# 112 unread f16 matmuls into spare PSUM columns, in front of 27 instructions of the attention stage

## The chip, the cores and the metric

The kernel runs on one core of a Trainium2 chip. The time is that of the device, in microseconds (us), from launch to end; less is better. TensorE (PE) does the matmuls and the transposes, VectorE (DVE), ScalarE (ACT) and GpSimd (POOL) work on their results, and SyncE (SP) issues transfers. TensorE's clock is granted at one of two levels, 1.2 or 2.4 GHz; the profile gives it as a share of full speed, 0.50 or 1.00.

## The reference

Three layers follow each other. The first is attention over 32 landmarks for each of 64 heads (8 batches of 8), with six Newton steps for an inverse; the second sends each token to one of eight experts; the third is a feed-forward layer.

```python
q_lm = q.reshape(B, H, m, S // m, D).mean(axis=3)      # m = 32, S = 576, D = 64
k_lm = k.reshape(B, H, m, S // m, D).mean(axis=3)
A, Bm, C = sm(q, k_lm), sm(q_lm, k_lm), sm(q_lm, k)    # softmax of the scaled products
Z = Bm.T / (norm1(Bm) * norminf(Bm) + 1e-06)
for _ in range(6):
    Z = 2 * Z - Z @ Bm @ Z
x = A @ Z @ C @ v
...
out[mask] = gate_w[mask, None] * (np.maximum(x[mask] @ w1[e], 0) @ w2[e])
...
h = np.maximum(x @ w_in, 0.0)
y = h * h @ w_out
```

## The kernel before

`phase_a` is the attention stage. Its work on a batch is split into parts written as generators: `front` turns q and k with TensorE (tiles `pt`, to `qT` and `kT`) and sums the landmarks on VectorE (`lms`); `head` makes the block matrices `bd` and `klm` from them and the small product `nb<-klm,bd`, its softmax, its transpose `BT` and the start `u` of the Newton steps; `mid` makes the products `pc` with the keys, their exponentials `eC`, transposes them (`pe`, to `eT`) and multiplies by v into `pv`; `newton` has the steps `nb<-u`, then `uc` and the two products with `Bm` and `wgt`; `amap` is the softmax over the landmarks of q (`pa`, `A`, `AT`); `xout` makes the logits of the router (`nb<-AT,G`, read into `lg`) and the stage's rows (`px`); `rout` finds each token's expert on VectorE (`mxl`, `eq`, `m`, `oh`, `ohv`), with the small products `pr` on TensorE.

The table `WHEN` gives every step of a part a due time in units of one batch, and the steps of all eight batches are written out in the order of those times, so that several batches are in work at once. A scheduler then sorts each engine's instructions once more, by when it thinks that they are ready. The later stages are written under a manual schedule and keep the order of the code. Every engine works through its own queue strictly in order: an instruction that waits holds all behind it.

PSUM has eight banks of 512 f32 columns. Six of them rotate as `big`; `nb` is one bank; `pv` is one bank, of which `mid` uses columns 0 to 127 alone. VectorE reads them into `u` (L491) when the product with v is done:

```python
V.tensor_tensor(s["u"][:, :, 32:96], pv[:, 0:128].rearrange("p (q d) -> p q d", q=2),
                rs.rearrange("p (q o) -> p q o", o=1).to_broadcast([128, 2, 64]), op=ALU.mult)
```

Of the kernel before, what the change touches and what calls it, by code (L numbers as in the profile page):

```python
# [8 lines left out]
F16 = mybir.dt.float16  # L9
# [42 lines left out]
            xout7=(1.731, 1.829))  # L52


def rowscale(nc, al, out, src, k, tag):

    m = al(tag)
    nc.vector.tensor_reduce(out=m, in_=src, axis=AX.X, op=ALU.max, apply_absolute_value=True)
    nc.vector.tensor_scalar(m, m, 2.0 ** -100, None, op0=ALU.max)
    mi = m.bitcast(I32)  # L60
    nc.vector.tensor_scalar(mi, mi, 0x7F800000, None, op0=ALU.bitwise_and)
    nc.vector.tensor_scalar(out.bitcast(I32), mi, -1.0, float((254 + k) << 23), op0=ALU.mult, op1=ALU.add)
# [6 lines left out]
             pt=([128, 8, 128], F16), ph=([128, 4, 128], F32), py=([128, DM], F32),  # L69
             sq=([128, 2], F32), s4=([128, 4], F32), jk=([128, DM], mybir.dt.bfloat16), iv=([128, 1], F32), gs=([128, 1], F32),  # L70
             sqy=([128, 2], F32), s4y=([128, 4], F32))


class Layer1:


    def __init__(self, nc, cst, wb, x2, al):
        self.nc, self.identh, self.x2, self.al = nc, cst["identh"], x2, al
        self.w1 = [wb[:, 0, i].rearrange("p (c f) -> p c f", c=4) for i in (0, 1)]
        self.w2 = [wb[:, 1, i].rearrange("p (c f) -> p c f", c=8) for i in (0, 1)]  # L80
# [6 lines left out]
    def prep(self, s):  # L87
        nc, al = self.nc, self.al
        xg = s.pop("xg")
        s["s1"] = s1 = al("s1")  # L90
        rowscale(nc, al, s1, xg[:, 0:DM], 3, "xm")
        yield
        s["xh"] = xh = al("xh")
        nc.scalar.activation(xh[:, 0], xg[:, 0:DM], AF.Copy, scale=s1[:, 0:1])
        yield
        nc.vector.scalar_tensor_tensor(xh[:, 1], xg[:, 0:DM], s1[:, 0:1], xh[:, 0], op0=ALU.mult, op1=ALU.subtract)
        s["gt"] = al("gt")
        nc.vector.tensor_copy(s["gt"], xg[:, DM:XW])
# [44 lines left out]
    def post(self, s, to, tok):  # L143

        nc, al = self.nc, self.al
        yg = al("yg")
        nc.scalar.activation(yg, s["py"], AF.Copy, scale=s["gt"][:, 0:1])
        yield
        s2 = al("s2")
        rowscale(nc, al, s2, yg, 3, "ym")  # L150
        yield
        xr = al("xr")
        nc.scalar.activation(xr[:, 0:DM], yg, AF.Copy, scale=s2[:, 0:1])
        yield

        ss = al("ss")
        nc.vector.tensor_tensor(ss, s["s1"], s2, op=ALU.mult)
        nc.vector.reciprocal(ss, ss)
        nc.vector.tensor_copy(xr[:, 2 * DM + 2:XD].bitcast(I32), tok)
        nc.vector.tensor_scalar(xr[:, 2 * DM:2 * DM + 2].bitcast(F32), ss, ss[:, 0:1], 2.0 ** -34, op0=ALU.mult, op1=ALU.mult)  # L160
        nc.vector.scalar_tensor_tensor(xr[:, DM:2 * DM], yg, s2[:, 0:1], xr[:, 0:DM], op0=ALU.mult, op1=ALU.subtract)
        nc.gpsimd.indirect_dma_start(out=self.x2, out_offset=bass.IndirectOffsetOnAxis(ap=to, axis=0),
                                     in_=xr, in_offset=None)
# [80 lines left out]
def phase_a(tc, cst, q, k, v, wg, x_rows, x2, ro, rt, w12, wb, held):  # L244
    nc = tc.nc
    V, P, ACT, PE = nc.vector, nc.gpsimd, nc.scalar, nc.tensor
    with (
# [17 lines left out]
        nb = psn.tile([128, 512], F32, name="nb")  # L265
        pv = psn.tile([128, 512], F32, name="pv")
        turns = [0, 0]
        sel3 = a1.tile([PR, LM], F32, name="sel3")
        P.memset(sel3, 1.0)
        P.affine_select(out=sel3, in_=sel3, pattern=[[-3, LM]], compare_op=ALU.is_ge, fill=0.0, base=0, channel_multiplier=1)  # L270
# [1251 lines left out]
def moe_kernel(tc, q, k, v, wg, w1, w2, win, wout, out, x_rows, x2):  # L1522
    nc = tc.nc
    with tc.tile_pool(name="cst", bufs=1, reuse_waits="tile") as cp:
# [14 lines left out]
        with tc.tile_pool(name="ro", bufs=1, reuse_waits="tile") as rp:  # L1539
            ro = consts_r(nc, rp)  # L1540
            phase_a(tc, cst, q, k, v, wg, x_rows, x2, ro, rt, (w1, w2), wb, held)
# [57 lines left out]
```

## Time and profile before

| what | value |
| --- | --- |
| median of three runs | 1370.7 us (1363.55 to 1373.35) |
| the profiled execution's own time | 1377.05 us |
| its span, first to last instruction | 1375.3 us |
| mean granted clock of TensorE | 0.975 |
| TensorE busy | 1318.0 us, 96% of the span |
| VectorE busy | 998.5 us, 73% |
| ScalarE busy | 737.6 us, 54% |
| GpSimd busy | 569.9 us, 41% |

The span is cut into stretches to be read: one engine's share of the whole says little, since the attention stage (to about 275 us) and the two stages behind it have different limits. TensorE's matmuls overlap in the records, and their ends are modelled, so a rate is read from many of them in a row and not from the duration of one. Where a row names what ended an idle time, "issue" means that the profile shows nothing that the engine waited for.

### The profile page before, as it was taken

What the parts mean: (1) busy time and instruction counts of PE and PEld (TensorE: products, weight loads), DVE (VectorE), ACT (ScalarE), POOL (GpSimd) and SP (SyncE); (2) the same over time, 40 slices, a digit from 0 to 9 for tenths busy, and PEclk for the clock granted to TensorE, in tenths of its full rate; (3) what the DMA queues carried; (4) which work ended last, traced back from release to release, by engine and by line L of the source; (5) the groups of instructions that cost most, each with busy time, mean ns of one, the idle gap of its engine ahead of it and who ended that gap; (6) DMA issues with size and microseconds to landing.
All of it is one profiled execution on the core that took longest, in us unless ns stands there. A gap on an engine that the chain in (4) does not pass through costs nothing.

```text
span 1375.3 us, 41268 instructions
## 1 busy us (share of the span) xinstructions
PE 1318.0 (96%) x16606; PEld 1081.4 (79%) x16606; DVE 998.5 (73%) x2654; ACT 737.6 (54%) x1387; POOL 569.9 (41%) x585
## 2 busy tenths in 40 slices
PE   5889988899999999999999999999999999999997
PEld 4556555577777777777588999999999999999996
DVE  5788788885678568886379777667777777777765
ACT  4445555443666456654355555555555555555554
POOL 4334455212344345564200244444444444444443
PEclk9799798999999999999999999999999999999999
DMA  9576676247486757564211211111111101111100
GB/s 207 124 189 153 152 178 146 76 152 184 140 245 186 178 118 229 145 133 111 61 27 32 32 33 24 25 33 33 32 33 32 32 18 32 33 33 32 25 9 32
DMA packets 132591, 126.94 MB, mean 92 GB/s; under 512 B 89760, under 2 KB 108192, under 8 KB 132384
## 3 DMA queue, kind: packets, MB, share of 16 engines
q1 hardware_dynamic: 122624, 94.19, 30.2%
q0 software_dynamic: 9120, 29.95, 6.7%
q8 instruction: 133, 2.18, 0.7%
q14 instruction: 74, 0.61, 0.2%
q10 hardware_dynamic: 640, 0.02, 0.0%
HBM read 215.03 MB, written 28.89 MB: 177 GB/s over the span
## 4 chain that ended last, share of the span: by engine, by line
PE 46%; DMA 2%; issue 1%; DVE 1%; ACT 1%; POOL 0%; POOLq 0%; ACTq 0%; DVEq 0%
PE o L1419 22%; PE h L1380 7%; PE h L1381 7%; PE h L1379 7%; DMA x<-xr,sidx 2%; PE h L1348 1%; PE h L1349 1%; PE h L1347 1%; DVE q L1385 1%; PE py L139 1%; ACT hq L1406 0%; ACT q L1399 0%; DVE out L1385 0%; DVE rr L1385 0%; ACT q L1400 0%
## 5 line engine op out<-in xcount | busy, mean ns | idle before, releaser
L1411 POOL TENSOR_TENSOR hq<-q,hq 128x896 f16<-128x896 f32 x127 | 239.8, 1888 | 308.4 <-ACT hq L1406 234.8
L1419 PE MATMUL o<-wo,hq 128*128 128x256 f16 x3024 | 355.6, 273 | 1.2 <-DVE hq L1411 0.7
L1419 PEld LDWEIGHTS <-hq 128*128 128x128 f16 x3024 | 290.1, 98 | 35.6 <-DVE hq L1411 1.0
L1385 DVE TENSOR_TENSOR q<-h,q 128x256 f32<-128x256 f32 x508 | 186.5, 388 | 136.3 <-ACT q L1394 110.3
L1399 ACT ACTIVATE q<-q 128x512 f32<-128x512 f32 x127 | 80.1, 630 | 220.7 <-DVE q L1385 220.7
L139 PE MATMUL py<-wb,hT 128*128 128x512 f16 x864 | 194.2, 381 | 2.4 <-ACTq L1042 2.2
L124 PE MATMUL ph<-xT,wb 128*128 128x128 f16 x1120 | 189.4, 219 | 1.9 <-DMA xT<-xh 1.9
L125 PE MATMUL ph<-xT,wb 128*128 128x128 f16 x1120 | 189.4, 219 | 0.0
L126 PE MATMUL ph<-xT,wb 128*128 128x128 f16 x1120 | 189.4, 219 | 0.0
L139 PEld LDWEIGHTS <-hT 128*128 128x128 f16 x864 | 83.5, 98 | 97.6 <-issue 5.2
L1406 ACT ACTIVATE hq<-q 128x896 f16<-128x896 f32 x144 | 136.0, 944 | 26.8 <-DVE q L1339 22.0
L1379 PE MATMUL h<-sx,wb 128*128 128x128 f16 x762 | 134.2, 219 | 0.8 <-DVE q L1385 0.8
L1380 PE MATMUL h<-sx,wb 128*128 128x128 f16 x762 | 134.2, 219 | 0.0
L1381 PE MATMUL h<-sx,wb 128*128 128x128 f16 x762 | 134.2, 219 | 0.0
L124 PEld LDWEIGHTS <-wb 128*128 128x128 f16 x1216 | 119.0, 98 | 6.2 <-ACTq L1042 2.1
L125 PEld LDWEIGHTS <-wb 128*128 128x128 f16 x1216 | 119.0, 98 | 4.9 <-issue 0.6
L126 PEld LDWEIGHTS <-wb 128*128 128x128 f16 x1216 | 119.0, 98 | 0.1
L130 DVE SCALAR_TENSOR_TENSOR hT<-ph,hT 128x512 f16<-128x512 f32 x72 | 49.6, 689 | 86.4 <-ACT hT L129 62.5
L129 ACT ACTIVATE hT<-ph 128x512 f16<-128x512 f32 x72 | 42.9, 595 | 127.3 <-PE ph L126 124.5
L1380 PEld LDWEIGHTS <-wb 128*128 128x128 f16 x1016 | 99.5, 98 | 0.9 <-issue 0.9
L1381 PEld LDWEIGHTS <-wb 128*128 128x128 f16 x1016 | 99.5, 98 | 0.0
L1379 PEld LDWEIGHTS <-wb 128*128 128x128 f16 x1016 | 99.5, 98 | 0.0
(348 smaller groups left out, 3182.5 us busy)
## 6 DMA issues: line engine op xcount, KB each, us to landing
stg<-in_moe_w SPq DMA_DIRECT2D x74, 2048.0 KB
qn<-in_q SPq DMA_DIRECT2D x16, 576.0 KB
kn<-in_k SPq DMA_DIRECT2D x16, 576.0 KB
vn<-in_v SPq DMA_DIRECT2D x16, 576.0 KB
fw<-in_moe_w_in SPq DMA_DIRECT2D x16, 512.0 KB
fw<-in_moe_w_out SPq DMA_DIRECT2D x16, 512.0 KB
x_rows<-xr SPq DMA_DIRECT2D x32, 192.0 KB
stg<-in_moe_w SPq DMA_DIRECT2D x16, 256.0 KB
```

Of the source, the lines that this page charges most:

```text
L124: nc.tensor.matmul(ph[:, f4], wh[:, c, fs], xT[:, c], start=(c == 0), stop=False)
L125: nc.tensor.matmul(ph[:, f4], wh[:, c, fs], xT[:, 4 + c], start=False, stop=False)
L126: nc.tensor.matmul(ph[:, f4], wl[:, c, fs], xT[:, c], start=False, stop=(c == 3))
L139: self.nc.tensor.matmul(py, hT[:, a, f], w[:, f], start=(i == 0), stop=(i == len(ps) - 1))
L1379: PE.matmul(ph[:, k], w(0, c), x(0, c), start=(c == 0), stop=False)
L1380: PE.matmul(ph[:, k], w(0, c), x(1, c), start=False, stop=False)
L1381: PE.matmul(ph[:, k], w(1, c), x(0, c), start=False, stop=(c == 1))
L1385: V.tensor_tensor(to, x, y, op=ALU.add)
L1399: ACT.activation(q[:, 3:7], q[:, 3:7], AF.Relu, scale=2.0 ** -8)
L1406: ACT.activation(hq[:, 0], s["q"], AF.Copy)
L1411: e.tensor_tensor(hq[:, 1], q, hq[:, 0], op=ALU.subtract)
L1419: PE.matmul(sums[k][:, z], hq[:, u, a], wo[:, x, f, w], start=(f == 0 and i == 0 and z == 0), stop=(f == 7 and i == 2), skip_group_check=True)
```

## The change

Each call of `matmul` and `transpose` in `phase_a` now goes through a small class that counts them. Where the count stands in the table `FEED`, it first issues that many matmuls of 128 by 128 weights (the f16 identity) on 384 columns of ones, into columns 128 to 511 of the bank of `pv`, which nothing reads. One more of them, with `start=True`, stands at the stage's beginning, with a `memset` of the ones on VectorE. Each is tied behind the instruction of TensorE that was written just before it; the scheduler may still put other instructions between the two. All calls that go through the class carry its line, L89, in the changed program.

```diff
+FEED = {70: 1, 152: 4, 208: 5, 216: 7, 276: 1, 474: 2, 503: 2, 538: 1, 589: 8, 604: 6, 797: 4, 895: 7, 926:
+            1, 982: 5, 988: 2, 1126: 10, 1131: 2, 1329: 2, 1348: 5, 1399: 10, 1454: 2, 1656: 3, 1765: 2, 1854:
+            2, 1856: 3, 1871: 13, 1893: 2}
...
+class Fed:
...
+    def call(self, f, *a, **k):
+        for _ in range(FEED.get(self.n, 0)):
+            self.feed()
+        self.n += 1
+        return f(*a, **k)
...
         pv = psn.tile([128, 512], F32, name="pv")
         turns = [0, 0]
+        ones = a1.tile([128, 384], F16, name="ones")
+        V.memset(ones, 1.0)
+        PE.matmul(pv[:, 128:512], cst["identh"], ones, start=True, stop=True)
+
+        def feed():
+            i = nc.tensor.matmul(pv[:, 128:512], cst["identh"], ones, start=False, stop=True, skip_group_check=True)
+            tc.keep_in_program_order(i)
+        PE = Fed(nc.tensor, feed)
```

The scheduler sorts the stage anew around them. In the sixth batch TensorE's queue came from the last Newton step of the batch before straight to the products with the keys, which read `bd`:

```order
L506 MATMUL nb<-u_2461 32x96 x8
L458 MATMUL pc_2630<-kT,bd_156 64x288
L382 MATMUL nb<-klm,bd_156 64x32 x4
L458 MATMUL pc_2630<-kT,bd_156 64x288
L458 MATMUL pc_2637<-kT,bd_156 64x288 x2
```

Now ten of the new matmuls, each with its load of weights (one pair of the ten is shown, and one of the two behind `nb<-klm`), stand there:

```order
L89 MATMUL nb<-u_2520 32x96 x8
L297 LDWEIGHTS identh
L297 MATMUL pv<-ones,identh 128x384
...
L89 MATMUL nb<-klm,bd_156 64x32 x4
...
L89 MATMUL pc_2701<-kT,bd_156 64x288 x2
L89 MATMUL pc_2708<-kT,bd_156 64x288 x2
```

The products with the keys, which stood first, now come behind `nb<-klm` and two more of the new matmuls; the second and the seventh batch have the same swap, the seventh with six matmuls there.

In the third batch TensorE went from the product that reads `m` (of the router for the first batch) to a Newton step on the `u` that VectorE makes from `pv`, and then to the router's counts `pr`:

```order
L638 MATMUL nb<-m,sel 128x1
L506 MATMUL nb<-u_1005 32x96 x8
L652 LDWEIGHTS tri
L652 MATMUL pr<-oh,tri 96x48
```

Now eight of the new matmuls follow (one pair is shown), then the counts, and the Newton step has moved behind those:

```order
L89 MATMUL nb<-m,sel 128x1
L297 LDWEIGHTS identh
L297 MATMUL pv<-ones,identh 128x384
...
L89 LDWEIGHTS tri
L89 MATMUL pr<-oh,tri 96x48
...
L89 MATMUL nb<-u_1026 32x96 x8
```

The first of the eight carries a wait for VectorE: it writes the bank that VectorE reads for `u` (L491). Six more stand behind the Newton step, in front of `nb<-AT,G`, and no other of the 112 carries a wait.

On VectorE the router's steps for the second batch stood behind `bd` and `klm` of the fourth, which TensorE reads:

```order
L564 TENSOR_REDUCE am<-A 128x18
L374 TENSOR_SCALAR bd_156<-lms 64x8x32 x2
L377 TENSOR_SCALAR klm<-lms 128x128
L621 TENSOR_REDUCE mxl<-lg 96x6
L512 TENSOR_TENSOR u_1495<-u_1473,nb 128x2x64
L624 TENSOR_TENSOR eq<-lg,mxl 96x48
```

Now they stand ahead of both (the rows between `m` and `bd` are left out):

```order
L653 TENSOR_REDUCE mxl<-lg 96x6
L656 TENSOR_TENSOR eq<-lg,mxl 96x48
L657 TENSOR_TENSOR lg<-lg,mxl 96x6x8
L660 TENSOR_TENSOR eq<-eq,ev 96x48
...
L664 TENSOR_REDUCE m<-eq 96x6
...
L406 TENSOR_SCALAR bd_156<-lms 64x8x32 x2
L409 TENSOR_SCALAR klm<-lms 128x128
```

Five small instructions have passed in front of the two that write `bd`. Elsewhere the same kinds of instructions have moved by some places, on every engine; the instructions themselves are the same.

## Rows read from the trace of the kernel before

**Rows 1.** The page: busy time by engine, and TensorE's clock in 40 slices.

```profile
PE 1318.0 (96%) x16606; PEld 1081.4 (79%) x16606; DVE 998.5 (73%) x2654; ACT 737.6 (54%) x1387; POOL 569.9 (41%) x585
...
PEclk9799798999999999999999999999999999999999
```

**Rows 2.** Windows: length, PE, PEld, DVE, ACT, POOL busy, clock, DMA share, GB/s.

```profile
25.90:275.00 249.10, 223.75 (x3123) 141.39 (x3120) 205.87 (x689) 128.95 (x340) 106.06 (x93) 0.88 0.64 148
...
36.10:53.20 17.10, 14.95 (x125) 9.54 (x125) 10.98 (x30) 5.11 (x14) 5.21 (x4) 0.50 0.94 210
...
94.10:101.00 6.90, 6.01 (x33) 3.29 (x33) 5.23 (x20) 1.16 (x3) 0.57 (x1) 0.51 1.11 251
...
124.90:131.70 6.80, 6.80 (x44) 3.92 (x43) 5.46 (x19) 3.48 (x7) 5.04 (x6) 0.50 0.99 218
...
152.20:169.20 17.00, 17.00 (x188) 11.21 (x177) 10.86 (x32) 7.04 (x16) 8.38 (x7) 0.50 0.41 97
...
176.10:179.50 3.40, 3.40 (x17) 1.70 (x17) 2.59 (x11) 1.75 (x7) 1.35 (x2) 0.50 1.10 252
...
203.40:206.80 3.40, 3.40 (x23) 2.12 (x23) 2.48 (x7) 1.40 (x4) 0.00 (x0) 0.50 0.55 150
...
227.30:234.10 6.80, 6.80 (x68) 5.11 (x69) 4.33 (x10) 4.29 (x9) 4.36 (x6) 0.50 0.66 113
...
330.00:660.00 330.00, 327.78 (x3725) 239.29 (x3723) 237.93 (x424) 188.13 (x333) 152.71 (x248) 1.00 0.63 161
```

**Rows 3.** Waits of TensorE, 25 to 275 us: total, times, longest.

```profile
PE pc L458 <- DVE bd L374: 6.3, 4, 2.0
PE nb L506 <- DVE lg L592: 2.8, 1, 2.8
...
PE pv L483 <- issue: 1.4, 1, 1.4
```

**Rows 4.** Timeline of TensorE: start, length, instruction, count, idle before and what ended it.

```profile
36.20 0.44 PE L483 MATMUL pv<-vn,eT 96*32 96x64 f32 x7 [1.42 <-issue]
...
93.25 0.53 PE L506 MATMUL nb<-u 32*32 32x96 f32 x16 [1.62 <-DVE u L491]
94.99 0.28 PE L652 MATMUL pr<-oh,tri 96*96 96x48 f16 x1 [1.21 <-DVE oh L644]
...
98.49 1.50 PE L589 MATMUL nb<-AT,G 128*32 128x192 f32 x12
...
175.97 1.10 PE L458 MATMUL pc<-kT,bd 128*64 128x288 f32 x2 [2.00 <-DVE bd L374]
...
196.40 0.85 PE L589 MATMUL nb<-AT,G 128*32 128x192 f32 x12 [1.06 <-DVE u L512]
...
202.39 0.53 PE L506 MATMUL nb<-u 32*32 32x96 f32 x16 [2.80 <-DVE lg L592]
...
209.78 0.67 PE L458 MATMUL pc<-kT,bd 128*64 128x288 f32 x2 [1.77 <-DVE bd L374]
...
226.14 0.43 PE L539 MATMUL nb<-wgt,WT 32*32 32x8 f32 x24 [0.64 <-issue]
```

**Rows 5.** The same timeline, in the stage behind: f16 matmuls of 512 columns in a row.

```profile
282.43 4.05 PE L139 MATMUL py<-wb,zkn 128*128 128x512 f16 x18
```

**Rows 6.** VectorE's groups, 25 to 275 us: busy, mean ns of one, idle before.

```profile
L377 DVE TENSOR_SCALAR klm<-lms 128x128 f32<-128x128 f32 x7 | 3.0, 424 | 0.1
L625 DVE TENSOR_TENSOR lg<-lg,mxl 96x48 f32<-96x48 f32 x7 | 2.3, 335 | 0.1
L624 DVE TENSOR_TENSOR eq<-lg,mxl 96x48 f32<-96x48 f32 x8 | 1.6, 196 | 0.1
L621 DVE TENSOR_REDUCE mxl<-lg 96x6 f32<-96x48 f32 x8 | 1.5, 184 | 0.0
L628 DVE TENSOR_TENSOR eq<-eq,ev 96x48 f32<-96x48 f32 x7 | 1.3, 192 | 0.0
L632 DVE TENSOR_REDUCE m<-eq 96x6 f32<-96x48 f32 x7 | 1.3, 185 | 0.1
```

**Rows 7.** Waits of VectorE, 25 to 275 us.

```profile
DVE u L512 <- ACT u L511: 9.1, 11, 1.9
DVE lms L355 <- ACT kT L352: 6.2, 8, 1.7
DVE G L542 <- PE nb L539: 3.9, 5, 2.0
```

More of the change, by code (lines that the diff above doesn't have):

```diff
@@ L71, with __init__, matmul, transpose @@
              sqy=([128, 2], F32), s4y=([128, 4], F32))
+class Fed:
+    def __init__(self, pe, feed):
+        self.pe, self.feed, self.n = pe, feed, 0
+    def call(self, f, *a, **k):
[3 more added lines that the diff above has]
+        return f(*a, **k)
+    def matmul(self, *a, **k):
+        return self.call(self.pe.matmul, *a, **k)
+    def transpose(self, *a, **k):
+        return self.call(self.pe.transpose, *a, **k)
 class Layer1:
```

## The prediction

> **What bounds the kernel now.** I read the page first: TensorE is busy for 96% of the span, and its clock dips only in the first 7 of 40 slices [rows 1]. The windows then split the span. From 330 to 660 us TensorE is busy for 327.78 of 330 us at full clock, and VectorE for 237.93 [rows 2]: this stage is TensorE's, nothing of it is edited, and what the attention stage ends earlier or later should pass through it whole. From 25.9 to 275 us the picture is mixed: of 249.1 us TensorE is busy for 223.75 and VectorE for 205.87, at a mean clock of 0.88 [rows 2]. So TensorE stands for 249.1 - 223.75 = 25.4 us there, nearly all of it behind VectorE: 6.3 us for `bd`, 2.8 for `lg`, and so on; one pause of 1.4 us, and one of 0.64, have no visible cause [rows 3, 4].
>
> The mean of 0.88 hides seven stretches at the lower level, 17.1 + 6.9 + 6.8 + 17.0 + 3.4 + 3.4 + 6.8 = 61.4 us in all [rows 2]. Five of them begin within a few us of a pause of TensorE that the rows show: 1.42 us before 36.20, 1.62 before 93.25, 2.00 before 175.97, 2.80 before 202.39, 0.64 before 226.14 [rows 4]. A pause alone doesn't decide it: the one of 1.77 us before 209.78 has no fall behind it [rows 4]. In these stretches TensorE is the late engine: it is busy for all 17.00 us of the fourth while VectorE has 10.86 us of work [rows 2], and VectorE's own waits are largely for results that come through TensorE, such as 6.2 us for `kT` and 3.9 for `nb` [rows 7].
>
> **The change, part by part.** *What a full clock would give.* The same twelve matmuls `nb<-AT,G` take 1.50 us in a slow stretch and 0.85 in a fast one [rows 4], a ratio of 1.76. TensorE's busy time in the seven stretches is 14.95 + 6.01 + 6.80 + 17.00 + 3.40 + 3.40 + 6.80 = 58.4 us; by that ratio it would be 33.1, a saving of 25 us if TensorE alone counted. It doesn't: VectorE has 10.98 + 5.23 + 5.46 + 10.86 + 2.59 + 2.48 + 4.33 = 41.9 us of work there [rows 2], and its work doesn't shrink, so at most 61.4 - 41.9 = 19.5 us can go. In the stage's other 187.7 us VectorE is busy for 205.87 - 41.9 = 163.9, or 87%. If the seven stretches become as dense as that, they take 41.9 / 0.873 = 48.0 us and 13.4 us are saved. I take 13.4 as the worth of all seven falls, with 0 and 19.5 as ends.
>
> *How many falls go.* Most blocks of new matmuls stand directly ahead of instructions that wait for VectorE, such as the ten ahead of the sixth batch's `nb<-klm`, where the pause was 2.00 us [rows 4]. Two doubts remain. The first of the long stretches begins behind a pause that ended by "issue" [rows 4]: no dependence sets it, so it can come elsewhere among the new instructions. And a faster TensorE reaches VectorE's results earlier, so it will pause where it did not pause before and where no block stands. I take two thirds of the worth: 13.4 x 2/3 = 8.9 us gained.
>
> *What the matmuls cost.* None of this kind is in the trace before. The nearest row is 18 f16 matmuls of 512 columns, each with its own weights, in 4.05 us at full clock [rows 5]: 0.225 us each, so 0.225 x 384/512 = 0.169 us for one of 384, and 112 x 0.169 = 18.9 us. At half clock the ratio above makes it 33 us. The lower bound is 0, if all lie inside pauses: 18.9 is less than the 25.4 us that TensorE stands. The Trainium skill ("TensorE: Matmul & The Clock Gate", section on the back-to-back issue gap) gives a sustained 131 ns for each pair of a weight load and a matmul of 512 columns, and 81 ns for 128; an estimate from these two is some 0.114 us for 384, or 13 us for all. The 0.225 us of rows 5 speaks against that, so the trace's figure stands.
>
> What is not hidden is read from the order. Thirteen stand behind an instruction that waits, or in front of one that waits for TensorE's own work alone: two and six in front of `pc`, and five more singly or in pairs, at 13 x 0.169 = 2.2 us. In the third batch the eight wait themselves for the `u` that VectorE makes from `pv`, so they can't fill the 1.62 us before 93.25; they come in the pause of 1.21 us behind it [rows 4], which their 1.35 us exceed by 0.1. The six after them stand where no pause was: 1.0 us. In sum 3.3 us.
>
> *What the new order costs.* In the second, sixth and seventh batch `pc` now comes behind `nb<-klm` and so behind VectorE's `klm` of 0.424 us [rows 6]: 3 x 0.42 = 1.3 us. The five router instructions ahead of `bd` are 184 + 196 + 335 + 192 + 185 ns = 1.1 us [rows 6]. Both lie on the way to what TensorE waits for, and I charge them whole; the end below is 0, if `bd` had time to spare there. What else moved changes sides by single places, and I put it at 0, with 6 us either way: a quarter of the 25.4 us of pauses that the old order left. The `memset` and the first matmul lie at the stage's start, where TensorE still waits for its first data, and cost nothing; were that cover gone, one matmul is 0.169 us.
>
> **The sum.** Against the profiled execution's own 1377.05 us: -8.9 + 3.3 + 1.3 + 1.1 = -3.2, so 1373.9. That execution lies 6.3 us above the median of 1370.7, and the same sum on the median gives 1367.5; I forecast 1367.
>
> **Rivals.** *All falls go.* Every pause is filled, no new one brings the clock down, and VectorE keeps up: 13.4 to 19.5 us less, against costs of 3.3 or a little more. That is -10 to -16, or 1355 to 1361. For it: most blocks have about the length of the pause that they fill. Against it: VectorE at 87% leaves little to take.
>
> *VectorE takes it all.* The clock stays up, TensorE arrives earlier everywhere and waits longer for VectorE, and the stage keeps its length within 3 us: 1368 to 1374. For it: 61.4 us hold 41.9 us of VectorE's work and the pauses before `bd` and `lg` are VectorE's [rows 2, 3]. Against it: VectorE waits 3.9 us for `nb` and 6.2 for `kT`, which only a faster TensorE brings sooner [rows 7].
>
> *Slower: the blocks outlast the pauses.* The clock still falls in the same stretches, so that some 45 of the matmuls run there at 0.30 us, and the scheduler's new order has moved the pauses away from them. The whole price is then 18.9 + 45 x 0.13 = 24.7 us, of which the pauses still hide half: 12 us more, and with 2.4 us for the order 1385. It decides from the point at which fewer than a third of the falls go, since the gain (4.4 us) is then below the costs.
>
> *It doesn't do what it says.* The Trainium skill ("PSUM — Partial Sum Buffer", section on bank collisions) says that TensorE and VectorE must not be in one bank and the same 32 partitions at once, also at other columns, so that spare columns don't make the new matmuls free of VectorE. Worked out from rows: were all blocks, not eight matmuls, to wait for VectorE's reading of `pv`, the pauses would stay unfilled, every fall would stay, and the 18.9 us would come behind the pauses, some half of it on the path: 1370.7 + 9 = 1380. In the built order one block alone has such a wait, so this is unlikely.
>
> **How the numbers follow.** The forecast (-9 to +1) has 0.42; VectorE taking it all 0.23; all falls gone 0.20; slower by outlasting 0.12; late blocks 0.03. One per cent, 13.7 us, is about what a measurement of this kernel can tell from no change; that puts "faster" below 1357 and "slower" above 1384.4. Of "all falls gone" some two thirds lies below 1357, and of the forecast a little: 0.18. Of the slower cases about two thirds lies above 1384.4, with a little for an order that turns out badly: 0.12. The rest, 0.70, is within 1%. The range takes the forecast, VectorE's case, most of "all falls gone" and the near part of the slower ones, with 6 us for the order: 1350 to 1384.
>
> **What would show it.** In the profile after, the windows of the stage should show a mean clock clearly above 0.88, with four or five of the seven stretches gone, the one at the first "issue" pause the likeliest to stay. The new line's group should show 112 matmuls, some 19 us of TensorE's time. The waits for `bd` and `lg` should be shorter, since matmuls now stand in them, and VectorE's busy time should be the same within 1 us in a stage that is some 3 us shorter. VectorE's waits for `kT`, `nb` and `G` should shrink. In the third batch the pause before the new block should still be there, ended by L491's new line. The stage behind should be as long as before. The prediction is wrong if the clock's mean stays near 0.88, or if the clock rises and the stage's end doesn't move at all (VectorE's case), or if an order that I put at 0 is worth more than the clock.

## The result and the profile after

The changed kernel takes 1387.4 us (median of four runs, 1380.96 to 1390.39) against 1368.4 us of the kernel before in the same session (four runs, 1363.55 to 1373.35): 1.0131 times as long, with a 95% interval of 1.0095 to 1.0166. I had forecast 1367 us, with 1350 to 1384 as the range, and had given "slower by over 1%" 12 chances in 100. A second set of six runs gave 1.0123 (1.0088 to 1.0158).

The two profiles must be read with their place in these runs in mind. The execution of before that I had read took 1377.05 us, 4 us longer than any of the twelve runs that stand beside the second set (of the 113 runs of before beside the experiments, three are longer); that of the changed kernel took 1380.96, the shortest of its four. Side by side they differ by 4 us, where the medians differ by 19. So I took a second profile of each, and the one of before that the comparisons below use is `pin_before` (1364.1 us), which is the same kernel with its order held fast, as explained there.

First the windows of the changed kernel: the time ahead of the stage's window, the window, its stretches at the lower clock, and the stage behind.

```profile
0.00:25.90 25.90, 12.37 (x74) 10.44 (x76) 13.22 (x26) 8.65 (x16) 13.22 (x45) 0.80 0.96 216
25.90:275.00 249.10, 227.09 (x3244) 141.56 (x3241) 211.66 (x701) 129.22 (x341) 105.67 (x93) 0.96 0.63 151
90.50:93.90 3.40, 3.40 (x32) 2.00 (x30) 2.78 (x10) 0.23 (x1) 0.80 (x1) 0.50 1.06 267
131.40:134.80 3.40, 3.40 (x30) 2.23 (x22) 2.90 (x7) 1.09 (x3) 0.42 (x1) 0.50 0.10 22
151.90:162.20 10.30, 9.48 (x111) 6.29 (x111) 7.85 (x18) 3.68 (x8) 5.01 (x6) 0.50 0.42 100
268.00:271.40 3.40, 3.40 (x10) 2.44 (x9) 2.68 (x18) 2.92 (x6) 0.00 (x0) 0.50 0.30 82
319.20:326.00 6.80, 3.81 (x37) 3.84 (x38) 2.27 (x5) 0.00 (x0) 0.18 (x1) 0.50 1.04 222
330.00:660.00 330.00, 329.75 (x3734) 240.22 (x3733) 239.39 (x429) 188.97 (x335) 152.12 (x246) 1.00 0.61 162
```

Of the seven stretches of [rows 2], 61.4 us, four are left in this window, 20.5 us, and its mean clock is 0.96 instead of 0.88. So far the forecast holds. But two new stretches stand outside the window: some 10 us ahead of it (a mean clock of 0.80 from 0 to 25.9 us), and 6.8 us behind it, at 319.20, at the entry of the expert stage.

The same windows of `pin_before`, a more usual execution of the old order:

```profile
25.90:275.00 249.10, 223.23 (x3246) 142.25 (x3247) 215.62 (x742) 132.28 (x344) 106.27 (x93) 0.92 0.63 152
```

Here the clock is lower than in the changed kernel, 0.92 against 0.96, and yet VectorE gets through 742 instructions in these 249.1 us, against 701. The first expert tile (TensorE's first `ph`) starts at 265.8 us here and at 275.8 in the changed kernel. That is the result in small: the clock is higher, and the stage's work comes later. In the profile of before, at a clock of 0.88, VectorE had got through 689, so these numbers hang on the execution as well.

TensorE's waits in 25 to 275 us after, which answer to [rows 3]:

```profile
PE nb L89 <- DVE lg L624: 4.5, 2, 2.5
PE pe L89 <- ACT eC L496: 3.2, 4, 2.0
PE nb L89 <- DVE u L544: 2.7, 6, 0.6
...
PE pv L297 <- DVE u L523: 1.0, 1, 1.0
```

The wait for `bd`, 6.3 us and the largest before, has gone from the head of the list, as forecast; the one for `lg` has not shrunk but grown, from 2.8 to 4.5. The last row is the one wait of the new matmuls for VectorE. VectorE's waits in the same window, for [rows 7]:

```profile
DVE lms L387 <- ACT qT L384: 5.9, 8, 1.8
DVE u L544 <- PE nb L89: 4.8, 5, 1.5
DVE A L589 <- PE pa L89: 3.6, 10, 1.1
DVE u L544 <- ACT u L543: 3.5, 8, 1.2
```

I had expected these to shrink with a faster TensorE. The one for `G` did, and it is no longer among the largest. In all VectorE stands for 249.1 - 211.66 = 37.4 us of this window, against 43.2 in the profile of before and 33.5 in `pin_before`: less than in the slow execution, more than in the more usual one.

### The profile page after: what moved, and what is told of

Its sections match the earlier page's. It is cut to its first block, busy times and chain, and to the rows that moved or that the text cites. A ratio compares the mean times of both kernels' runs of the same rounds, so it can differ in the third digit from the quotient of the medians.

```text
span 1379.3 us, 41483 instructions
## 1 busy us (share of the span) xinstructions
PE 1322.1 (96%) x16719; PEld 1082.9 (79%) x16719; DVE 1003.7 (73%) x2655; ACT 736.5 (53%) x1387; POOL 569.3 (41%) x585
## 4 chain that ended last, share of the span: by engine, by line
PE 45%; DMA 2%; issue 1%; DVE 1%; ACT 1%; POOL 0%; POOLq 0%; ACTq 0%; DVEq 0%
PE o L1451 22%; PE h L1411 7%; PE h L1413 7%; PE h L1412 7%; DMA x<-xr,sidx 2%; PE h L1380 1%; PE h L1381 1%; PE h L1379 1%; DVE q L1417 1%; ACT hq L1438 0%; ACT q L1431 0%; DVE out L1417 0%; DVE rr L1417 0%; ACT q L1432 0%; POOL hq L1443 0%
```

## The experiments

The change does two things at once: it adds matmuls ("feeds" from here on), and it makes the scheduler sort the stage anew. To have each alone, a function behind the writing of the stage ties every instruction to the one that a list names as the one before it on its engine, with an order-only tie that adds no wait between engines. The list is the order that the scheduler gave one kernel or the other.

```diff
+ORDER = {"PE": ..., "DVE": ..., "Activation": ..., "Pool": ..., "SP": ...}
+def pin(tc, fed=(), own=None):
...
+        for a, b in zip(row, row[1:]):
+            tc.add_manual_dep(b, a.name, mybir.DependencyInfo(mybir.DependencyClass.NoSync, mybir.DependencyReason.DATA),
+                              reason="pin")
...
             trace(nm, b, i + 1)
+        pin(tc)
```

My theory was that the new order costs the time. Its rivals: the feeds outlast their pauses; or a shorter attention stage meets a busy DMA at the entry of the expert stage and loses there what it gained.

**after_again**: the changed kernel, unaltered.

> The changed kernel once more, unaltered, for a second profile beside the first, whose run was the shortest of its four. If its length is set in the attention stage (order of the instructions, or feeds that outlast their pauses), the router's counts come no earlier than in the profile of before and the expert stage is as long as it was. If it is lost behind the attention stage, the counts come 3 to 5 us earlier than before, as in the first profile, and the loss stands at the first expert tiles, with a wait for the transposing DMA (xT<-xh) of 5 us or more and a half-speed stretch of the clock behind it. Either way the ratio to before is 1.013, give or take 0.004.

1383.1 us, 1.0123 (1.0088 to 1.0158), clock 0.991 in the profile, that of the shortest of the six runs (their mean is 0.986). TensorE waits 3.3 us for `xT` at the entry of the expert stage, against 5.5 in the first profile, and no half-speed stretch follows. So the entry is not where most of the time goes.

**order_only**: the list of the changed kernel on the kernel before.

> No feeds, no ones tile; every instruction of the five engines is held in the order that the scheduler gave the changed kernel. If the new order costs the time: 1380 to 1390 us, ratio 1.010 to 1.016, clock falls as in before. If the feeds themselves cost it, or the entry of the expert stage that a shorter attention stage meets: within 4 us of before, 1364 to 1372 us; the prediction's own terms for the order (pc behind klm, five router instructions ahead of bd) give +2.4 us.

1387.6 us, 1.0147 (1.0106 to 1.0188), without a single feed. The new order alone costs what the change costs, and it takes no shorter attention stage for that. Also the clock is worse than before: the six runs have a mean of 0.976, the twelve of before 0.985.

**feeds_only**: all feeds, the list of before.

```diff
+    names = {i.name for i in fed} | {own.name if own else ""}
...
+        for r in struct.unpack(f"<{len(raw) // 2}H", raw):
+            row += [next(own_turn) for x in BLOCKS.get(r, ())] if e == "PE" and fed else []
```

`BLOCKS` gives for an instruction, by its number as written, how many feeds stand ahead of it.

> All 112 feeds ahead of the 27 instructions that the table names, and every other instruction of the five engines held in the order of the kernel before. If the new order costs the time: faster than before, by 5 to 9 us (the prediction's clock term, less some feeds that run past their pause), 1359 to 1364 us. If feeds that outlast their pauses cost it: 1380 to 1390 us, as the changed kernel. If the entry of the expert stage takes the gain and more: the router's counts come 3 to 8 us earlier than in before, the end 0 to 10 us later than this would give, 1364 to 1385 us, with the transposing DMA waited for 5 us or more.

1378.2 us, 1.0084 (1.0053 to 1.0114): slower, where my theory alone gives faster. The loss lies in the stage, whose first `ph` starts at 276.4 us, and TensorE has no wait of 5 us behind it. The feeds do what they are for, since the clock's mean is 0.991 over seven runs, the highest of all kernels here. But they stand in the wrong places. TensorE's timeline of this kernel, and then of `pin_before`, at the five feeds of the fifth batch:

```profile
147.25 0.42 PE L117 MATMUL nb<-u 32*32 32x64 f32 x16 [0.85 <-DVE u L499]
147.60 0.99 PE L325 MATMUL pv<-ones,identh 128*128 128x384 f16 x5
148.52 0.71 PE L117 MATMUL pa<-qT,bd 128*64 128x288 f32 x4
```

```profile
147.83 0.42 PE L535 MATMUL nb<-u 32*32 32x64 f32 x16 [0.81 <-DVE u L468]
148.19 0.71 PE L584 MATMUL pa<-qT,bd 128*64 128x288 f32 x4
```

The pause of 0.8 us stands ahead of `nb<-u`; the feeds stand behind it, ahead of a `pa` that followed without a pause, and `pa` begins 148.52 - 147.25 = 1.27 us behind `nb<-u` instead of 148.19 - 147.83 = 0.36: 0.91 us later for nothing. The table of the change names instructions that wait in the new order. In the old order nearly all of them don't, so the two belong together, and this run prices feeds without pauses and not the order.

**before_look** and **pin_before**: the kernel before once more, and with its own list.

> The kernel before once more, unaltered, for a second profile: the one shown was of its longest run (clock 0.975). If the length of a run goes with how often the clock falls in the attention stage, this one has a higher mean clock (0.98 to 0.99), a shorter attention stage (first expert tile some 5 to 12 us earlier than in the profile shown) and an unchanged rest.

1369.8 us with a clock of 0.981 (one run). The first `ph` starts at 269.6 us instead of 277.0, and the rest is as long as before (1098.5 and 1098.3 us): the shorter time goes with the higher clock, as expected.

> The kernel before with every engine's instructions held in the order that the scheduler gave them anyway: a control for the device of holding. Every theory expects the time of before, 1364 to 1371 us, ratio 0.998 to 1.002; more than that would mean that holding an order costs something by itself.

1364.9 us, 0.9975 (0.9954 to 0.9996). Holding an order costs nothing (the ratio lies just below the range that I had given), so the other lists can be read at their face value.

**order_attn** and **order_tail**: the new list to the stage's last batch and the old one behind, and the reverse.

Only the lists in `ORDER` differ from those of `order_only`; on TensorE they change over behind the 1717th instruction, on VectorE behind the 686th.

> No feeds. The changed kernel's order up to the last batch's reads of the state (TensorE's first 1717 traced instructions, VectorE's first 686), the order of before behind that. If the new order costs in the attention stage: most of the 20 us of order_only, 1378 to 1388 us. If it costs at the entry of the expert stage: 1364 to 1373 us.

> No feeds. The order of before up to the last batch, the changed kernel's order from there to the first expert tiles. If the new order costs in the attention stage: 1364 to 1372 us. If it costs at the entry of the expert stage (the profile of order_only has a wait of 4.0 us for VectorE's fg ahead of the first experts): 1378 to 1388 us.

1382.9 us, 1.0096 (1.0065 to 1.0127), and 1369.3 us, 1.0007 (0.9982 to 1.0031). Most of the cost, some 15 of 20 us, is made in the attention stage (`order_only` has some 5 us more than these two together, but the intervals of `order_only` and `order_attn` overlap); the new order of the router's tail and of the first experts costs nothing of itself. What does reach over is the wait of the first experts. TensorE's waits there, in the changed kernel, in `order_attn` and in `pin_before`:

```profile
PE ph L148 <- DMA xT<-xh: 5.5, 1, 5.5
```

```profile
PE ph L153 <- DVE fg L1262: 5.2, 1, 5.2
```

```profile
PE ph L153 <- ACTq L1072: 1.7, 1, 1.7
```

`order_attn` has the old list here and still waits 3.5 us longer than `pin_before`. So the new order upstream reaches this wait too; by which way, these rows don't tell.

**feeds_fit**: 73 feeds in the old order (its expectation says 72), as many as fit (at 0.17 us each) ahead of the 18 instructions behind a pause that three profiles of this order share.

```diff
-FEED = {70: 1, 152: 4, ...}
...
+BLOCKS = {..., 268: [0, 1, 2, 3, 4, 5], ..., 1859: [0, 1, ..., 12], ...}
```

> 72 feeds ahead of 18 instructions, in the pauses that three profiles of the order of before all show (0.39 to 2.32 us each, as many feeds as fit at 0.17 us); every other instruction in the order of before. If feeds cost only where they outlast a pause, and the clock pays 0.3 us for each us at half speed that they save (some 15 to 20 us fewer): 1360 to 1366 us, ratio 0.994 to 0.999. If a feed costs its 0.17 us wherever it stands: 12 us more and the clock's 5 less, 1372 to 1378 us.

1372.1 us, 1.0017 (0.9984 to 1.0049). The time stands at the lower edge of the second range, the ratio between the two. Feeds that lie in pauses cost nothing that can be measured, and gain nothing either: the clock's mean is 0.985 in these runs and 0.982 in those of before beside them, some 6 us fewer at half speed where I had expected 15 to 20. This was the version that might have beaten both kernels; it doesn't.

**order_others** and **order_sp**: the new list on all engines but TensorE, and on SyncE alone.

> No feeds. TensorE in the order of before; VectorE, ScalarE, GpSimd and SyncE in the order that the changed kernel has. If the cost of the new order is TensorE's own (its waits in another place): 1364 to 1372 us. If it is in the order of the four others: 1380 to 1390 us, as order_only.

> No feeds. Only SyncE's queue in the order of the changed kernel (loads of x and of the weights' staging, stores of the rows), the four others in that of before. If the order of the transfers carries the cost, the wait at the entry of the expert stage above all: 1372 to 1388 us. If it doesn't: 1364 to 1371 us, with 2 us or less of wait at the first experts, as in before.

1393.9 us, 1.0179 (1.0143 to 1.0215), and 1379.1 us, 1.0074 (1.0052 to 1.0096). By the times alone, TensorE's own new order isn't needed for the loss, and the order of SyncE's transfers is enough for half of it. But lists of two orders don't belong together, and that can cost time by itself. In `order_sp`, from 120 to 205 us, GpSimd waits for the load of an expert weight (`stg`), and VectorE stands as long for `A`, which comes behind it in GpSimd's queue:

```profile
POOL stg L730 <- DMA stg<-in_moe_w: 6.1, 1, 6.1
```

```profile
DVE AT L607 <- POOL A L605: 6.0, 1, 6.0
```

Where all lists are new (`order_only`, `order_attn`, the changed kernel) or all old (`pin_before`), VectorE waits 0.7 to 1.3 us for this `A` in the whole stage. So these two runs don't tell which engine's order carries the loss of the change.

**order_early** and **order_late**: the new list up to the fifth batch's scores, or from there to the last batch; the old one elsewhere.

> No feeds. The changed kernel's order up to the fifth batch's scores (TensorE's first 939 traced instructions, VectorE's first 363, some 142 us into the program), the order of before behind that. If the loss grows evenly with the moved instructions: half of order_attn's 15 us, 1374 to 1378 us. If it is made in batches 5 and 6, as the profiles of the changed kernel and of order_attn show it (the fourth batch's read of pv is within 3 us of the held kernel of before, the sixth 9 to 12 us late): 1366 to 1371 us.

> No feeds. The order of before up to the fifth batch's scores, the changed kernel's order from there to the last batch, the order of before behind that. If the loss grows evenly: 1374 to 1378 us. If it is made in batches 5 and 6: 1377 to 1385 us, with VectorE some 2 to 3 us less busy in each 35 us from 130 to 200 us than in the held kernel of before, and the sixth batch's read of pv 7 us or more late.

1377.0 us, 1.0076 (1.0046 to 1.0106), and 1391.5 us, 1.0194 (1.0149 to 1.024). The first lies in the range of an even growth, the second above both of its ranges. Together that is 2.7%, where the whole of `order_attn` costs 1.0%: two orders joined by hand have a seam, and these two runs can't split the loss. `order_late` has the wait of `order_sp` again, and longer. Its timeline, of GpSimd and then of VectorE:

```profile
168.51 0.62 POOL L730 TENSOR_SCALAR stg<-stg 128x512 f32<-128x512 f32 x1 [7.46 <-DMA stg<-in_moe_w]
169.10 1.16 POOL L605 TENSOR_TENSOR A<-A,ar 128x576 f32<-128x576 f32 x1
```

```profile
170.29 0.78 DVE L607 STREAM_TRANSPOSE AT<-A 128x576 f32<-128x576 f32 x1 [8.71 <-POOL A L605]
```

GpSimd's queue has the scaling of an expert weight (`stg`) ahead of a step of the softmax (`A`). It waits 7.46 us for the load of that weight, and VectorE, which wants `A`, stands for 8.71 us behind a transfer that attention doesn't need.

**feed_late**, **feed_early** and **feed_ones**: the changed kernel with a part of its table, each with an order that the scheduler made in one piece. (`feed_late` has 71 feeds and not the 62 that its expectation names.)

```diff
-FEED = {70: 1, 152: 4, ..., 1893: 2}
+FEED = {895: 7, 926: 1, ..., 1893: 2}      # feed_late
+FEED = {70: 1, 152: 4, ..., 797: 4}        # feed_early
+FEED = {70: 1, 152: 1, ..., 1893: 1}       # feed_ones
```

> The changed kernel with the feeds of the table's first eleven places left out: 62 feeds, all from the fifth batch on, and the scheduler's own order, which is that of before up to TensorE's 902nd row. If the loss is made by the order in batches 5 to 8: 1376 to 1386 us, ratio 1.006 to 1.013. If it needs the moves of the first batches as well: 1364 to 1372 us.

> The changed kernel with the first eleven places' feeds alone (41 of them for the first four batches); the scheduler's order differs from that of before in all eight batches, since what comes later is planned anew. If feeds of the late batches cost the time: 1364 to 1372 us. If the new order costs it, whatever feeds stand in it: 1376 to 1388 us.

> One feed instead of 1 to 13 at each of the 27 places, 27 in all and some 4.6 us of TensorE's time, with a third order of the scheduler's own (355 of TensorE's rows moved against 482). If only the particular order of the changed kernel is bad, or its many feeds: 1364 to 1373 us. If any newly planned order costs, since the one before was the outlier: 1374 to 1388 us.

1378.5 us, 1.0068 (1.0046 to 1.0091); 1376.4 us, 1.0063 (1.0038 to 1.0089); 1374.8 us, 1.0046 (1.0024 to 1.0069). That the first two add up to the whole (0.68 + 0.63 = 1.31%) proves little, since the order of `feed_early` differs from that of before in all eight batches. The third order, with a quarter of the feeds, costs too, at the low end of what I had said for it. Each of the four orders that the scheduler planned anew was slower than the one before.

**late_bare**: the order of `feed_late`, without its feeds.

> No feeds. Every engine in the order that the scheduler gave feed_late, which is that of before for the first four batches and has no seam made by hand. If the order costs the time by making VectorE wait in batches 5 and 6: 1376 to 1386 us, with VectorE busy for 59 to 62 us of 135 to 205 us (the held kernel of before: 66.84) and its waits there 6 us or more (2.3). If the 71 feeds of feed_late cost it: 1364 to 1371 us, VectorE as busy as in before.

1382.9 us, 1.0101 (1.007 to 1.0132): slower than with the feeds (the longest run of `feed_late` is about the shortest of these). Its lists are the old ones up to TensorE's 901st instruction and VectorE's 322nd. Windows from 135 to 205 us (columns as in [rows 2]), of `pin_before`, `late_bare`, `feed_late` and the changed kernel:

```profile
135.00:205.00 70.00, 58.54 (x834) 36.12 (x834) 66.84 (x199) 39.20 (x103) 39.69 (x37) 0.95 0.72 177
```

```profile
135.00:205.00 70.00, 60.52 (x768) 36.73 (x765) 57.05 (x171) 35.26 (x91) 35.48 (x34) 0.85 0.72 168
```

```profile
135.00:205.00 70.00, 62.30 (x846) 37.63 (x844) 60.46 (x180) 38.09 (x97) 36.70 (x34) 0.98 0.70 169
```

```profile
135.00:205.00 70.00, 63.66 (x840) 39.15 (x832) 58.76 (x180) 37.18 (x96) 35.79 (x34) 0.93 0.68 165
```

In `pin_before` VectorE is busy for 66.84 of these 70 us, 95%, and does 199 instructions. TensorE's waits there, 11.3 us in sum, are all for VectorE, so VectorE sets the pace in this stretch. In the three others it does 171 to 180 instructions, and stands for 9.5 to 13 us instead of 3. But the old order isn't always as dense as this. The same window in the profile of before, and in `feed_ones`, a slower kernel with an order planned anew:

```profile
135.00:205.00 70.00, 61.02 (x811) 38.70 (x810) 58.81 (x180) 36.92 (x96) 35.38 (x33) 0.84 0.70 166
```

```profile
135.00:205.00 70.00, 60.80 (x856) 38.27 (x857) 65.28 (x196) 38.87 (x99) 37.72 (x35) 0.95 0.71 177
```

At a clock of 0.84 the old order leaves VectorE no busier than the new ones, and `feed_ones` comes close to `pin_before`. The clock of `late_bare` is 0.85 here, so its row alone doesn't part the order from the clock. `feed_late` does so better, at 0.98, but its feeds take TensorE's time too. VectorE's waits in this stretch, in `pin_before`, in before, and the largest in `late_bare`:

```profile
DVE m L489 <- PE pc L487: 0.7, 3, 0.3
DVE u L541 <- PE nb L535: 0.5, 1, 0.5
```

```profile
DVE u L512 <- ACT u L511: 3.3, 3, 1.7
DVE G L542 <- PE nb L539: 2.0, 1, 2.0
```

```profile
DVE A L586 <- PE pa L584: 3.9, 3, 2.6
DVE lms L384 <- ACT qT L381: 2.2, 3, 1.3
DVE G L571 <- PE nb L568: 1.9, 2, 1.1
```

A fairer pair has the same mean clock, no feeds, and lists that are joined in the last batch only: `order_tail`, with the old order up to there, and `order_attn`, with the new one. From the start to TensorE's first `ph`:

```profile
0.00:265.60 265.60, 224.76 (x3208) 144.11 (x3209) 221.49 (x728) 139.11 (x358) 119.36 (x138) 0.94 0.69 162
```

```profile
0.00:276.20 276.20, 226.46 (x3207) 144.06 (x3208) 225.84 (x722) 137.14 (x356) 119.04 (x138) 0.94 0.65 154
```

The new order takes 10.6 us longer for about the same instructions, at a clock of 0.94 in both. VectorE stands for 50.4 us instead of 44.1, 6.3 more, and is busy for 4.4 us more; why the same instructions keep it busy longer isn't shown. As one profile stands for each, and any engine stands longer in a longer stage, this gives the size of the loss and speaks against the clock, but it doesn't show that VectorE's waits are the first cause.

## Why the prediction was wrong

**The step that failed** is the last of the part on the new order: "What else moved changes sides by single places, and I put it at 0, with 6 us either way". With the two terms that I did charge the order stood at 2.4 us. It measured 20 us in `order_only` (1387.6 against 1367.4). Of these, some 8 are the clock. Within the twelve runs of before, spans go from 1358.4 us at a mean clock of 0.994 to 1371.2 at 0.980. Read as time at half speed (twice the clock's shortfall times the span) that is 16 and 55 us, so 12.8 / 39 = 0.33 us for each (a straight line through all 113 runs of before has a slope of 0.34). This is an estimate, from runs that may differ in more than the clock. `order_only` stands at 0.976 or 66 us, before at 0.985 or 42, and 24 x 0.33 = 8. The other 12 us belong to the order at an equal clock: 10.6 us of it show between `order_tail` and `order_attn`. In these VectorE stands some 6 us longer and is busy some 4 us longer. I had named the case ("if an order that I put at 0 is worth more than the clock") and priced it from the wrong place: a quarter of TensorE's pauses, although a new order can also make VectorE stand.

**That VectorE is the limit** I had seen as "87%", a mean over the stage's stretches at full clock. In `pin_before` it is 95% from 135 to 205 us, in the profile of before 84%. That filling TensorE's pauses was therefore of little use there, and making VectorE wait dear, is an argument from these shares and not a measurement.

**The clock's term** was right in kind for the feeds, and in size by some luck: in the new order, from `order_only` to `after_again`, the mean clock goes from 0.976 to 0.986, or from 66 to 39 us at half speed, worth 27 x 0.33 = 9 us; I had said 8.9, but from 41 us fewer (two thirds of 61.4) at 0.22 us each (13.4 / 61.4). Besides, the new order had taken nearly as much beforehand: the ten runs of the changed kernel have a mean of 0.985, and so have the twelve of before. Against the old kernel the term is about 0. The profile had hidden this, since its 61.4 us at half speed were more than the usual execution has in the whole program (42).

**The feeds' term** held, as far as the noise lets it be told. The times go from 1387.6 to 1383.1 us, 4.5 us of gain, but the runs of the two kernels overlap; with 9 from the clock the feeds cost some 4.5, and the forecast was 3.3. The gain is clearer from `late_bare` to `feed_late`, one order without and with 71 feeds: 1382.9 and 1378.5 us, at mean clocks of 0.979 and 0.984. Where feeds lie in a pause they are nearly free, and where not they cost about their length. TensorE's timeline of `order_only`, then of the changed kernel, at the ten feeds of the sixth batch:

```profile
175.06 0.64 PE L411 MATMUL nb<-klm,bd 128*64 128x32 f32 x8 [2.10 <-DVE u L541]
```

```profile
170.51 1.80 PE L297 MATMUL pv<-ones,identh 128*128 128x384 f16 x10
172.68 0.42 PE L89 MATMUL nb<-klm,bd 128*64 128x32 f32 x8 [0.37 <-DVE u L544]
```

Ten feeds fill 1.80 us of a pause of 2.10 us. And the thirteen near the end of the stage, in `order_only` (without them) and in the changed kernel:

```profile
277.16 1.89 PE L628 MATMUL px<-wbd,AT 128*128 128x256 f32 x8
```

```profile
270.42 1.29 PE L89 MATMUL px<-wbd,AT 128*96 128x256 f32 x3
271.54 2.28 PE L297 MATMUL pv<-ones,identh 128*128 128x384 f16 x13
273.65 0.59 PE L89 MATMUL px<-wbd,AT 128*96 128x256 f32 x2
```

They stand between `px` and `px`, where TensorE has no wait, and take 273.65 - 271.54 = 2.1 us of its time. The prediction's 3.3 us had left this block out. Both rows agree with the price of 0.169 us that I took from 512 columns: 1.80 / 10 = 0.18, 2.28 / 13 = 0.175. In the old order, nearly all without a pause (`feeds_only`), they come near their whole price of 18.9 us: 11 us slower at a clock that is 0.006 better, 17 us at half speed, worth 5 to 6, so 16 to 17 us.

**That a gain would "pass through it whole"** to the stage behind was too simple. The wait at the first experts grew from 1.7 to 3.3 and 5.5 us in the two profiles, and in `order_attn` to 5.2, where no instruction of this place had moved. Such a wait is a few us of the 19.

**The rivals.** "The blocks outlast the pauses" gave 1385, and that is near the time, but not the mechanism: without any feed the time is the same or longer. "Late blocks", by which reading `pv` would keep the feeds back, showed in one group, 1.0 us in the third batch, as the built order said. "VectorE takes it all" has no run to itself: `feeds_fit`, which filled the old order's pauses, hardly raised the clock.

What stays open is which of the several hundred moves make the stage longer. The runs with lists of two orders can't tell, since such a mixture can cost time by itself. That the five queues fit each other less well in a newly planned order is a reading that all runs allow, but it is argued and not shown: no run has taken a single move by itself.

## What to carry to other kernels

An edit that makes a scheduler sort a dense stage anew is two edits, and the second can be several times the first: hold the old order, or run the new order without the edit, before explaining the edit itself. Compare orders at an equal clock, and in more than one execution: one profile of the old order here looked as slow as the new ones. Look for the engine that has the least slack in the stretch, and ask of every move whether that engine now waits; a mean over a stage hides it. Unread matmuls can raise the clock and still cost more than it gives back, as in `feeds_only`.

## What the runs showed of the hardware

Within one kernel, 39 us more at the lower clock go with 12.8 us more of time, 0.33 us for each. TensorE's own matmuls lose more: by `nb<-AT,G`, 1.50 us at the lower clock and 0.85 at full, 0.43 of each such us. That the other engines set part of the pace would explain the difference, but no run shows it by itself.

One kernel's mean clock differs from run to run: 0.974 to 0.994 over the 113 runs of before. Feeds in the pauses that recur didn't hold it up reliably: the twelve runs of `feeds_fit` go from 0.975 to 0.993. The 112 feeds of `feeds_only` did, with 0.989 to 0.993 in seven runs, at the price told above.

An in-order queue passes a late transfer on: the load that GpSimd awaited for 7.46 us made VectorE stand for 8.71, which doesn't touch that weight (`order_late`).
